# Linear attention and Sinkhorn-routed experts on one core: the attention front moved beside expert 0, and the expert loop turned outside in

## The chip, the cores and the metric

The kernel runs on one core of a Trainium2 chip. The metric is the device time of one execution in microseconds (us). The times of whole kernels are medians of executions; times within a kernel come from its one profiled execution. The engines are PE (TensorE, matmuls), PEld (its weight loads), DVE (VectorE), ACT (ScalarE), POOL (GpSimd) and SP (SyncE, here only an issuer of DMAs). SBUF is the working memory on the chip; the results of matmuls go to PSUM, here in banks of 128x512 fp32 values, and VectorE or ScalarE moves them from there to SBUF, which is called evicting. The granted clock is the share of TensorE's full clock that the profile shows as let through.

## The reference, cut to what matters

```python
q, k, v: (8 batches, 8 heads, 576, 64) fp32      # x below has N = 4608 rows of 512
phi(x) = where(x > 0, x, exp(x) - 1) + 1
kv  = einsum('bhsd,bhse->bhde', phi(k), v);  z = sum_s phi(k)
x   = einsum(phi(q), kv) / (einsum(phi(q), z) + 1e-6)     # heads side by side
P   = exp(x @ w_gate - max)                               # (4608, 8)
for _ in range(8):                                        # Sinkhorn
    P /= P.sum(1, keepdims=True) + 1e-9
    P /= P.sum(0, keepdims=True) + 1e-9
    P *= N / E
for e in range(8):                                        # every expert sees every row
    out += P[:, e:e+1] * (max(x @ w1[e], 0) @ w2[e])      # 512 -> 1024 -> 512
```

The experts are nearly all of the arithmetic: 8 experts, 9 groups of 512 rows, and 64 matmuls of 128x512 for each pair (32 that make `hq = x @ w1`, 32 that make `ye = relu(hq) @ w2`). `phi` of k is computed in both kernels as max(x + 1, exp(min(x, 0))): a min on VectorE, an exp on ScalarE, a max on VectorE. The changed kernel does q the same way.

## The kernel before

It has a front, the Sinkhorn iterations and an expert part, one after the other, and a scheduler orders the instructions. The front:

```python
for b in range(B):
    ...                                   # q: cast by DMA to DRAM as fp16, then a transposing DMA
    for rq in range(NR // 2):
        nc.sync.dma_start(out=k_q, ...)                       # fp32, runs of 256 bytes
        nc.gpsimd.dma_start(out=v_q[:, :, 0:D], ...)          # cast to fp16 on the way
        ...                                                   # phi of k
    for r in range(NR):
        ...                                                   # kv, num/den, division, transpose of x
```

The expert part takes three groups at a time and runs all experts over them, so that weights are loaded three times:

```python
for sg in range(NSG):                    # 3 supergroups
    for e in range(E):
        ...                              # load w1[e], w2[e]
        for gi in range(GSG):            # 3 groups of 512 rows
            ...                          # 32 hq and 32 ye matmuls, Relu on ScalarE
            for tt in range(4):          # ye has ONE set of four PSUM banks
                nc.vector.scalar_tensor_tensor(out=oacc[gi][:, tt, :], in0=ye_ps[:, tt, :],
                                               scalar=P_sb[:, gg, e:e + 1], in1=oacc[gi][:, tt, :], ...)
```

The softmax here doesn't subtract the row's maximum and nothing guards it: scores larger than these inputs give would overflow.

## Time and profile before

| what | before |
|---|---|
| time, median of 2 | 1229.8 us (1229.6 to 1229.99) |
| span of the profiled execution | 1228.2 us |
| front, to about | 204 us |
| period of one group of 64 matmuls | 13.97 us |
| PE busy | 89% of the span |
| granted clock, mean | 0.998 |
| read from HBM | 129 MB |

Three rows of the table of 40 slices on the page (each digit is a slice of 30.7 us, in tenths busy; GB/s is what the DMA engines moved):

```profile
PE   0162378999999999999999999999999999999997
...
DMA  9999991043044214433440343044434413440301
GB/s 163 161 150 161 157 106 11 1 69 63 6 69 69 44 25 69 69 91 81 69 69 5 65 69 57 13 69 73 100 68 69 69 18 52 69 69 3 67 31 73
```

Six slices in which DMA is at 9 and PE is between 0 and 7, then PE at 9 to the end. The front is about a sixth of the time, and it has DMA engines that are busy while they move only some 160 GB/s.

### The profile page before, as it was taken

What the parts mean: (1) busy time and instruction counts of PE and PEld (TensorE: products, weight loads), DVE (VectorE), ACT (ScalarE), POOL (GpSimd) and SP (SyncE); (2) the same over time, 40 slices, a digit from 0 to 9 for tenths busy, and PEclk for the clock granted to TensorE, in tenths of its full rate; (3) what the DMA queues carried; (4) which work ended last, traced back from release to release, by engine and by line L of the source; (5) the groups of instructions that cost most, each with busy time, mean ns of one, the idle gap of its engine ahead of it and who ended that gap; (6) DMA issues with size and microseconds to landing.
All of it is one profiled execution on the core that took longest, in us unless ns stands there. A gap on an engine that the chain in (4) does not pass through costs nothing.

```text
span 1228.2 us, 13108 instructions
## 1 busy us (share of the span) xinstructions
PE 1093.9 (89%) x5568; PEld 490.8 (40%) x5568; DVE 328.4 (27%) x634; ACT 415.1 (34%) x642; POOL 107.9 (9%) x119
## 2 busy tenths in 40 slices
PE   0162378999999999999999999999999999999997
PEld 0142255344444444444444444444444444444442
DVE  3264484831121111221112211122111221111211
ACT  2253332333333333333333333333333333333332
POOL 7461020000000000000000000000000000000000
PEclk9999999999999999999999999999999999999999
DMA  9999991043044214433440343044434413440301
GB/s 163 161 150 161 157 106 11 1 69 63 6 69 69 44 25 69 69 91 81 69 69 5 65 69 57 13 69 73 100 68 69 69 18 52 69 69 3 67 31 73
DMA packets 173274, 84.21 MB, mean 69 GB/s; under 512 B 131744, under 2 KB 156320, under 8 KB 173216
## 3 DMA queue, kind: packets, MB, share of 16 engines
q0 software_dynamic: 112656, 59.78, 38.5%
q1 hardware_dynamic: 60560, 23.60, 10.7%
q8 instruction: 43, 0.70, 0.2%
q14 instruction: 15, 0.12, 0.0%
HBM read 128.99 MB, written 14.16 MB: 117 GB/s over the span
## 4 chain that ended last, share of the span: by engine, by line
PE 81%; issue 6%; DMA 6%; POOL 4%; DVE 3%; ACT 0%; DVEq 0%; POOLq 0%; ACTq 0%
PE ye_ps L300 40%; PE hq L290 39%; DMA v<-in_v_dram 6%; POOL q L93 2%; POOL v L131 1%; DVE yst L309 0%; DVE gsum L246 0%; PE logits_ps L211 0%; POOL v L133 0%; DVE w_tmp L232 0%; DVE w_tmp L244 0%; DVE ut L235 0%; PE csum_ps L247 0%; PE num_ps L171 0%; DVE t L242 0%
## 5 line engine op out<-in xcount | busy, mean ns | idle before, releaser
L296 ACT ACTIVATE h_sb<-hq 128x512 f16<-128x512 f32 x576 | 343.7, 597 | 669.2 <-PE hq L290 669.2
L290 PE MATMUL hq<-xT,w_t 128*128 128x512 f16 x2208 | 524.6, 379 | 0.0
L300 PE MATMUL ye_ps<-w_t,h_sb 128*128 128x512 f16 x2208 | 523.1, 380 | 0.3 <-ACT h_sb L296 0.3
L315 DVE SCALAR_TENSOR_TENSOR oacc<-ye_ps,P_sb,oacc 128x512 f32<-128x512 f32 x252 | 171.8, 745 | 707.8 <-PE ye_ps L300 707.8
L300 PEld LDWEIGHTS <-h_sb 128*128 128x128 f16 x2304 | 205.0, 98 | 301.2 <-ACT h_sb L296 113.7
L290 PEld LDWEIGHTS <-w_t 128*128 128x128 f16 x2208 | 215.2, 97 | 264.3 <-issue 11.3
L158 PE MATMUL kv_ps<-v,kp_q 128*64 128x65 f16 (+1 forms) x320 | 24.8, 249 | 104.4 <-POOL v L133 103.9
L280 POOL DMA_DIRECT2D w_t<-in_moe_w_dram x23 | 17.3, 753 | 886.7 <-PE hq L290 886.7
L158 PEld LDWEIGHTS <-kp_q 128*64 128x64 f16 (+1 forms) x320 | 19.8, 143 | 108.9 <-issue 97.8
L93 POOL DMA_DIRECT2D q<-in_q_dram x32 | 45.1, 2792 | 0.2 <-issue 0.2
L201 ACT COPY xT<-xT_ps 128x576 f16<-128x576 f16 x32 | 20.2, 637 | 72.0 <-PE xT_ps L196 71.8
L196 PE MATMUL xT_ps<-ident,x_sb 128*128 128x128 f16 (+1 forms) x160 | 24.5, 292 | 16.6 <-DVE x_sb L187 7.8
L171 PE MATMUL num_ps<-kv_sb,qpTg 64*128 64x65 f16 (+1 forms) x320 | 35.2, 244 | 0.8 <-DVE kv_sb L165 0.8
L311 DVE TENSOR_SCALAR oacc<-ye_ps,P_sb 128x512 f32<-128x512 f32 x24 | 16.4, 744 | 67.5 <-PE ye_ps L300 67.5
L103 ACT ACTIVATE qT1g<-qTg 128x2304 f16<-128x2304 f16 x8 | 17.0, 2124 | 33.6 <-DMA qTg<-q 33.6
L187 DVE TENSOR_TENSOR x_sb<-num_ps,rden 128x320 f16<-128x320 f32 x64 | 27.8, 480 | 0.1
L171 PEld LDWEIGHTS <-qpTg 64*128 64x128 f16 (+1 forms) x320 | 24.0, 121 | 9.5 <-issue 0.9
L142 ACT ACTIVATE e_k<-m_k 128x1152 f16<-128x1152 f16 x16 | 18.4, 1164 | 23.3 <-DVE m_k L140 21.2
L131 POOL DMA_DIRECT2D v<-in_v_dram x16 | 25.1, 1571 | 3.5 <-POOL v L133 3.2
L300 PE MATMUL ye_ps<-w_pre,h_sb 128*128 128x512 f16 x96 | 25.0, 391 | 0.0
L196 PEld LDWEIGHTS <-x_sb 128*128 128x128 f16 (+1 forms) x160 | 14.3, 125 | 25.5 <-issue 12.2
L290 PE MATMUL hq<-xT,w_pre 128*128 128x512 f16 x96 | 24.4, 400 | 0.0
(50 smaller groups left out, 192.9 us busy)
## 6 DMA issues: line engine op xcount, KB each, us to landing
w_t<-in_moe_w_dram POOLq DMA_DIRECT2D x46, 1024.0 KB, 11.4
k<-in_k_dram SPq DMA_DIRECT2D x16, 576.0 KB, 11.2
out_dram<-oacc SPq DMA_DIRECT2D x9, 1024.0 KB, 5.1
q<-in_q_dram POOLq DMA_DIRECT2D x32, 144.0 KB, 13.7
v<-in_v_dram POOLq DMA_DIRECT2D x16, 288.0 KB, 12.9
w_pre<-in_moe_w_dram POOLq DMA_DIRECT2D x2, 1024.0 KB, 17.0
qTg<-q SPq DMA_TRANSPOSE x8, 13.4
wg_sb<-in_moe_w_gate_dram POOLq DMA_DIRECT2D x1, 8.0 KB, 4.7
```

Source lines behind the costliest of these rows:

```text
L93: nc.gpsimd.dma_start(out=q16[bq][ds(rq * S, S), :].rearrange("s (h d) -> s h d", h=2), in_=AP(tensor=q.tensor, offset=(bq * H + 2 * rq) * ...
L131: nc.gpsimd.dma_start(out=v_q[:, :, 0:D], in_=AP(tensor=v.tensor, offset=base, ap=[[D, P], [P * D, NJ2], [1, D]]))
L142: nc.scalar.activation(out=e_k, in_=m_k, func=AF.Exp)
L158: nc.tensor.matmul(kv_ps[64 * hh:64 * hh + 64, :], lhsT=kp_sb[r0:r1, j, :], rhs=v1_sb[r0:r1, j, :], start=(ci == 0), stop=(ci == len(ch) - 1),
L171: nc.tensor.matmul(num_ps[0:cols, hh, m * 65:(m + 1) * 65], lhsT=qpT_sb[64 * hh:64 * hh + 64, 128 * m:128 * m + cols], rhs=kv_sb[64 * hh:6 ...
L187: nc.vector.tensor_tensor(out=x_sb[:, :, 64 * hh:64 * hh + 64], in0=numv, in1=rden[:, hh, :, None].broadcast_to([P, NM, D]), op=ALU.mult,)
L196: nc.tensor.transpose(xT_ps[:, 128 * m:128 * m + rows], x_sb[0:rows, m, :], ident[0:rows, 0:rows],)
L201: nc.scalar.copy(out=xT_sb[r][:, S * b:S * b + S], in_=xT_ps)
L290: nc.tensor.matmul(hq_t[fi], lhsT=w1_t[:, rr, ts(f, P)], rhs=xT_sb[rr][:, ds(512 * g, 512)], start=(rr == 0), stop=(rr == NDT - 1),)
L296: nc.scalar.activation(out=h_sb[:, fi, :], in_=hq_t[fi], func=AF.Relu)
L300: nc.tensor.matmul(ye_ps[:, tt, :], lhsT=h_sb[:, fi, ds(P * tt, P)], rhs=w2_t[:, f, :], start=(Qq == 0 and fi == 0), stop=(Qq == 3 and fi ...
L315: nc.vector.scalar_tensor_tensor(out=oacc[gi][:, tt, :], in0=ye_ps[:, tt, :], scalar=P_sb[:, gg, e:e + 1], in1=oacc[gi][:, tt, :], op0=ALU ...
```

## The change

Its intent is to take the front off the path. q, k and v come as large fp32 loads on the SP queue (each partition reads whole rows), GpSimd casts v, PE transposes phi(q). Only batch 0 stands alone. The other seven batches are emitted as a generator, in stages, between the matmul steps of expert 0, which runs unscaled because P isn't known yet. Sinkhorn follows as the last stages of the same generator; then the accumulators of expert 0 are scaled, and experts 1 to 7 run over all nine groups each, adding into accumulators that stay in SBUF. Weights are read once. The order of every queue is manual. The diff, cut to its core:

```diff
+    ctx.enter_context(tc.manual_schedule())
+    ye = [yps.tile([P, 512], FP32, tag=f"ye{t}", name=f"ye{t}") for t in range(4)]
 ...
-                nc.sync.dma_start(out=k_q, in_=AP(tensor=k.tensor, offset=base,
-                                                  ap=[[D, P], [P * D, NJ2], [1, D]]))
-                nc.gpsimd.dma_start(out=v_q[:, :, 0:D], ...)
+        src = [[NJ * D, P], [2 * S * D, 2], [1, NJ * D]]
+        for nm, ten in (("k", k), ("v", v), ("q", q)):
+            nc.sync.dma_start(out=t.rearrange("p r j d -> p r (j d)"), in_=AP(tensor=ten.tensor, offset=off, ap=src))
 ...
+    def att(b, g):                      # one half batch (4 heads), in 8 stages
+        kp = phi(kin, "k")
+        for hh in range(2):
+            nc.gpsimd.tensor_copy(out=vv[64 * hh:64 * hh + 64, :, :, hh, 0:D], in_=vin[64 * hh:64 * hh + 64])
+        qp = phi(qin, "q")
+        yield
+        ...                             # kv | transposes of q | den, num, division | transposes of x
 ...
+    def side_work():
+        for b in range(1, B):
+            pair = [att(b, 0), att(b, 1)]
+            ...                         # the two half batches stage by stage, in turn
+            if b % 2 == 1:
+                yield from logits(b // 2)
+        yield from sinkhorn()
 ...
+    def run(units, hqpool, look, after):
+        for i in range(len(steps) + look):
+            if i < len(steps):
+                steps[i][0](steps[i][2])                  # 4 hq matmuls and a Relu
+            if i >= look:
+                after(i - look)
+                steps[i - look][1](steps[i - look][2])    # 4 ye matmuls (and the evictions, at f = 7)
+    RATE = 2.4                                            # stages of side work for each step
+    run([(0, g, w1c, w2c) for g in range(7)], hq2, 1, after0)
+    while not side_done[0]:
+        advance()
 ...
+    for e in range(1, E):
+        run([(e, g, w1c, w2c) for g in range(NG)], hq4, 3, lambda i: None)
```

## The prediction

> **What bounds the kernel now.** I read the page's table of 40 slices first, then the chain of waits, the table by stage, the groups, and last the timeline at three places. The table by stage (columns: stretch in us; busy us of PE, its weight load, VectorE, ScalarE, GpSimd with counts; granted clock; DMA share; GB/s):
>
> ```profile
> 100.00:150.00 50.00, 14.18 (x150) 10.30 (x150) 16.31 (x44) 12.77 (x12) 6.70 (x9) 1.00 1.52 164
> ...
> 215.00:240.00 25.00, 23.03 (x108) 9.78 (x107) 20.70 (x66) 7.16 (x12) 0.00 (x0) 1.00 0.00 0
> ...
> 400.00:600.00 200.00, 199.84 (x916) 85.06 (x915) 38.17 (x56) 68.13 (x115) 8.18 (x10) 1.00 0.36 67
> ```
>
> There are two kernels in one. Up to about 204 us the attention front runs and its stretches show no compute engine even half busy, while the DMA queues are full (the share column is above 1) at only 164 GB/s. From 204 us to 1219 us the PE is solid. The chain of waits says the same by line:
>
> ```profile
> PE ye_ps L300 40%; PE hq L290 39%; DMA v<-in_v_dram 6%; POOL q L93 2%; POOL v L131 1%; DVE yst L309 0%; DVE gsum L246 0%; PE logits_ps L211 0%; POOL v L133 0%; DVE w_tmp L232 0%; DVE w_tmp L244 0%; DVE ut L235 0%; PE csum_ps L247 0%; PE num_ps L171 0%; DVE t L242 0%
> ```
>
> The front waits for v (fp32 cast to fp16 by GpSimd-issued DMA in 256-byte runs), for q's prepass and its DMA transpose; everything afterwards is the two expert matmuls. In the steady part, the groups repeat every 13.97 us (in the chain in order of time the 14 hq matmuls that open a group start at 408.26, 422.23 and 436.20), so 13.97 / 64 matmuls = 0.2183 us per 128x512 matmul, and 8 experts x 9 groups x 13.97 = 1005.8 us. Front 204 + 1006 + 9 lost in the first groups (sinkhorn steps and a cold clock) + 9 of tail (1219 to 1228) makes the 1228 us span.
>
> One detail of the steady part decides my prediction. The timeline at a group boundary:
>
> ```profile
> 604.20 2.73 DVE L315 SCALAR_TENSOR_TENSOR oacc<-ye_ps,P_sb,oacc 128x512 f32<-128x512 f32 x4 [11.24 <-PE ye_ps L300]
> ...
> 604.00 3.23 PE L290 MATMUL hq<-xT,w_t 128*128 128x512 f16 x14
> 607.07 1.89 PE L300 MATMUL ye_ps<-w_t,h_sb 128*128 128x512 f16 x8
> ```
>
> The four evictions of ye need 604.20 to 606.93; ye has only one set of four banks. The scheduler put 14 hq matmuls (3.07 us) there, so the next ye matmul at 607.07 just doesn't wait.
>
> **What the Trainium skill says.** (1) "TensorE: Matmul & The Clock Gate", section Back-to-back issue gap: N/2.4 + 2.5 ns when warm, 216 ns at N=512. The trace agrees within 1.5% (218), so this term can't shrink. (2) Same page, Part 1: after about 3.4 us of idling the array runs at half rate until it has been busy about as long. The trace agrees: eight matmuls below take 3.58 us, about 0.43 each, at the end of the sparse front.
>
> ```profile
> 204.43 3.58 PE L290 MATMUL hq<-xT,w_pre 128*128 128x512 f16 x8
> ```
>
> (3) "DMA: Bandwidth & Descriptors", section SWDGE vs HWDGE vs iDMA: a cast during DMA exists only on the GpSimd path. That is why the old v and q loads sit there; plain fp32 loads can go to the SP queue. The trace has the SP store of 1 MB at 262 GB/s including its ends (1222 to 1226 us), against 164 in the front. (4) "Perfetto Trace Analysis", section Matmuls: independent matmul groups should rotate through PSUM banks so that evacuation overlaps the next group. Neither kernel does it for ye; before replaces it by the 14 hq matmuls, above.
>
> **The change, part by part.** Its order of instructions is manual. I read it from the built program.
>
> *Experts 1 to 7.* 63 groups x 13.97 = 880 us as before. But hq now runs only three tiles ahead, and between the last four ye matmuls of a group and the first four of the next stand only 4 hq matmuls; the ye matmuls wait on VectorE. Let 0 be the start of the last ye matmul on bank 0. Matmul start to eviction start is 0.41 us (the fourth bank's in the same timeline the last eight ye start at 602.27 and take 1.90: 602.27 + 1.90 less one matmul's recorded 0.38 is 603.79, eviction 604.20). Four evictions in 2.73 us with 0.745 for the last are 0.66 apart, so bank k is free at 0.41 + 0.66k + 0.745 + 0.04 = 1.20, 1.86, 2.52, 3.18. PE would come to bank k at 8 x 0.218 + 0.218k = 1.75, 1.96, 2.18, 2.40. Banks 2 and 3 are late; the loss is 3.18 - 2.40 = 0.78 us. At an expert's first group 16 hq matmuls stand there and nothing is lost. 7 x 8 boundaries x 0.78 = 44 us. **Sum 924 us.**
>
> *Front for batch 0, exposed.* Six loads of 590 KB at an estimated 330 GB/s (a weight load at 296 to 310 us writes 151 GB/s x 14 us = 2.1 MB of fp16, so reads 4.2 MB of fp32, in 0.94 x 14 = 13.2 us: 320) land one each 1.8 us from about 4.5 us. VectorE then runs four phi in a row. Rows:
>
> ```profile
> L144 DVE SCALAR_TENSOR_TENSOR kp_q<-k,e_k 128x1152 f16<-128x1152 f32 x16 | 21.6, 1351 | 5.0 <-ACT e_k L142 5.0
> ...
> L142 ACT ACTIVATE e_k<-m_k 128x1152 f16<-128x1152 f16 x16 | 18.4, 1164 | 23.3 <-DVE m_k L140 21.2 <-DVE rden L182 2.1
> ```
>
> min 0.76 (median of L140) + exp 1.16 + max 1.4 (two halves) + handovers 0.1 = 3.4 us each, strictly in series because VectorE's order is min, max, min, max: 13.7 us, to about 18.5. Transposes of q, num/den, transposes of x through two PSUM buffers and 637 ns ScalarE copies: some 12 us. **31 us.**
>
> *Batches 1 to 7 beside expert 0.* PE work per batch: 6.67 of the 8-matmul steps (16 generator stages at 2.4 per step) x 1.75 = 11.7 us, plus an estimated 6.6 us of attention (per half batch 9 kv matmuls of 260 columns at 260/512 x 0.218 = 0.11, and 39 small matmuls and transposes at about 0.06, a quarter of 0.218 for 128 columns: 3.3): 18.3 us. If PE bound, 7 x 18.3 = 128 us. But the queues are in order, and the four exps of the next batch stand behind this batch's x copies and two Relus, which wait for PE: exp starts 5.6 us after the last division (two steps, four x transposes, a Relu). The four phi then take 12.7 us; the Relus of later steps stand behind them, with only two hq buffers, so PE has one more step and the kv matmuls to do and stops for about 10 us. After kv's copies (0.4) come the q transposes, den, num and four steps: 12.3 us. 5.6 + 12.7 + 0.4 + 12.3 = **31 us a batch, 217 for seven**; four logits rounds add 6.
>
> *Sinkhorn.* Now 8 VectorE operations between PE sums; from the rows of before (458, 453, 378, 458, 670, small ones about 0.2, PE handover 0.49) 3.9 us an iteration against 4.76 before, 31 us in all. Before hid it behind the PE stream; here 9 stages stand within under 4 steps, so PE waits at each sum. With the 4 steps left over (7 us): **38 us.**
>
> *Groups 7 and 8 of expert 0:* **28 us.** The 36 scalings of accumulators (about 0.4 each, 14.4 us) lie beside expert 1's first 14 us. *Tail:* eviction 3.1 and small stores, **7 us** against 9.
>
> Sum: 31 + 217 + 6 + 38 + 28 + 924 + 7 = **1251 us**. So the hiding of the front (saves most of 204) is paid back by stalls in expert 0, an exposed sinkhorn and the ye boundary.
>
> **Rivals.** *A: PE bound beside expert 0.* If phi overlaps more than I think, a batch takes 18 to 22 us: 1160 to 1190 us. For it: summed busy times per batch are only about 15 us for VectorE and ScalarE. Against: the program order. *B: cold clock.* Stops of 10 us per batch should send the array to half rate for 3 to 4 us after each (0.43 us seen above); 2 us x 8 more, 1265 to 1270, more if it stays cold throughout. *C: DMA or GpSimd.* 3.5 MB per batch is 11 us at 330 GB/s, hidden in 31; but at batch 1 they share with 8 MB of weight reads, perhaps 5 to 10 us once. No row of before shows a GpSimd copy of 64x1152; at 8 us each (four a batch) it would become the bound and make 1290. *D: no boundary loss.* If the evictions free banks earlier, 44 us fall away: 1207.
>
> **Range and chances.** 1251 with B pulling up and A down. My serial chain is built by hand, so I leave wide room below: 1195 to 1285. More than 2% faster means under 1205, which needs both A in part and D, or A fully: 0.18. Within 2%, 1205 to 1254: 0.40. Slower: 0.42.
>
> **What would show it.** Right: ye groups in experts 1 to 7 repeat every 14.75 us with ye idle "<-DVE acc"; first hq near 31 us; expert 0's seven groups end near 285 us with PE under 65% busy and Relus waiting behind exps; expert 1 starts near 320. Wrong: a 13.97 us period (step of the boundary false), or expert 0 done before 250 us (serial chain false), or PE waiting on GpSimd or DMA per batch.

## The result, and the profile after

The changed kernel takes **1266.84 us** (1266.49 to 1267.18, 2 runs) against 1229.8, and its result is right. The ratio is 1.030 with a 95% interval of 1.027 to 1.033: slower by 3%.

The same rows of the table of slices, for the changed kernel (a slice is 31.6 us; PEclk is the granted clock in tenths):

```profile
PE   3766667676999999999999999999999999999997
...
PEclk9877888886999999999999999999999999999999
DMA  9733322100210012000400040004000400003333
GB/s 271 199 113 112 109 97 73 60 1 1 46 21 1 1 19 48 1 1 1 67 1 1 1 67 1 1 1 67 1 1 1 67 1 1 1 1 67 67 77 90
```

The DMA bound is gone: 271 GB/s in the first slice, and a share of 3 or less in the third to tenth. PE starts at once, but it is at 6 or 7 for nine slices, at a granted clock of 0.6 to 0.8. The table by stage (columns as in the prediction: stretch, its length, PE, PEld, DVE, ACT and POOL busy with counts, clock, DMA share, GB/s) has one batch, the Sinkhorn and the experts:

```profile
105.00:140.00 35.00, 22.99 (x187) 12.93 (x186) 16.93 (x28) 13.84 (x22) 5.61 (x4) 0.80 0.31 102
280.00:320.00 40.00, 25.80 (x93) 11.39 (x94) 24.58 (x69) 7.04 (x12) 0.00 (x0) 0.70 0.00 1
500.00:900.00 400.00, 387.54 (x1760) 171.87 (x1759) 76.32 (x112) 131.32 (x220) 4.91 (x6) 1.00 0.10 16
```

In the batch no engine is busy for more than 23 of 35 us: it is bound by a chain that runs through all of them. In the experts PE is busy for 387.5 of 400 us, where before had 199.84 of 200. The timeline at a group boundary there answers to the one that the prediction shows of before (start, duration, engine, line, operation, count, and in brackets the idle time before it and what ended it):

```profile
706.80 2.73 DVE L289 SCALAR_TENSOR_TENSOR acc<-ye,P_sb,acc 128x512 f32<-128x512 f32 x4 [11.91 <-PE ye L274]
...
706.38 1.03 PE L274 MATMUL ye<-w,h 128*128 128x512 f16 x4
707.24 1.03 PE L265 MATMUL hq<-xT,w 128*128 128x512 f16 x4
708.11 0.59 PE L274 MATMUL ye<-w,h 128*128 128x512 f16 x2
708.92 0.38 PE L274 MATMUL ye<-w,h 128*128 128x512 f16 x1 [0.22 <-DVE acc L289]
709.58 0.38 PE L274 MATMUL ye<-w,h 128*128 128x512 f16 x1 [0.28 <-DVE acc L289]
```

Between the last ye matmuls of a group and the first of the next stand 4 hq matmuls, where before had 14. Banks 2 and 3 aren't yet evicted when PE comes to them. Undisturbed, the four starts would be 0.216 us apart, so the fourth would start at 708.11 + 0.65 = 708.76; it starts at 709.58. That is 0.82 us lost, although the bracketed idle times add up to only 0.50: a matmul's recorded duration (0.38) is longer than its spacing, and hides part of a wait.

The chain of waits by engine (its shares of the span) answers to that of before, of which the prediction shows the shares by line (PE had 81% there, DMA 6, DVE 3):

```profile
PE 73%; DVE 18%; issue 4%; ACT 4%; DVEq 0%; DMA 0%; ACTq 0%
```

DMA has left the chain, and VectorE has come in: half of its 18% are evictions at the boundaries, the rest phi, division and Sinkhorn.

The stages, read from where their first and last instructions stand, against the terms predicted:

| stage of the changed kernel | predicted | measured |
|---|---|---|
| batch 0, to the first hq | 31 | 34.0 |
| batches 1 to 7 with the logits | 217 + 6 | 243.3 (34.0 to 277.3) |
| Sinkhorn and the steps beside it | 38 | 36.4 (to 313.7) |
| groups 7 and 8 of expert 0 | 28 | 27.8 (to 341.5) |
| experts 1 to 7 | 924 | 916 (to 1257.4) |
| tail | 7 | 8.0 |
| sum | 1251 | 1265.4 (the span) |

In the same terms, before spends 63 x 13.97 = 880 us on all but nine groups, 9 in the tail, and so 1228.2 - 889 = 339 us on the front, the Sinkhorn and nine groups. The changed kernel needs 341.5 for these. **So the whole gain of hiding the front is lost again inside the first 341 us**, and the experts then cost 36 us more (916 against 880). The experiments ask where each loss sits.

### The profile page after: what moved, and what is told of

Same layout as the page of the kernel before. It is cut to its first block, busy times and chain, and to the rows that moved or that the text cites. A ratio compares the mean times of both kernels' runs of the same rounds, so it can differ in the third digit from the quotient of the medians.

```text
span 1265.4 us, 13555 instructions
## 1 busy us (share of the span) xinstructions
PE 1116.9 (88%) x5536; PEld 516.0 (41%) x5536; DVE 346.6 (27%) x587; ACT 427.3 (34%) x695; POOL 62.2 (5%) x63
## 4 chain that ended last, share of the span: by engine, by line
PE 73%; DVE 18%; issue 4%; ACT 4%; DVEq 0%; DMA 0%; ACTq 0%
PE hq L265 35%; PE ye L274 34%; DVE acc L289 9%; DVE pk L106 2%; ACT mk L103 1%; ACT mq L103 1%; DVE pq L106 1%; DVE xn L159 1%; DVE mq L102 1%; PE xt_ps L169 1%; PE qt_ps L139 1%; DVE mk L102 1%; ACT h L268 1%; PE num_ps L157 1%; PE kv_ps L128 1%
## 5 line engine op out<-in xcount | busy, mean ns | idle before, releaser
L274 PE MATMUL ye<-w,h 128*128 128x512 f16 x2304 | 616.1, 384 | 30.2 <-DVE acc L289 27.9
L265 PE MATMUL hq<-xT,w 128*128 128x512 f16 x2304 | 597.0, 384 | 0.0
L268 ACT ACTIVATE h<-hq 128x512 f16<-128x512 f32 x576 | 343.9, 597 | 732.0 <-PE hq L265 731.6
L289 DVE SCALAR_TENSOR_TENSOR acc<-ye,P_sb,acc 128x512 f32<-128x512 f32 x252 | 171.7, 744 | 731.2 <-PE ye L274 731.2
L265 PEld LDWEIGHTS <-w 128*128 128x128 f16 x2304 | 227.6, 99 | 304.3 <-issue 44.8
L274 PEld LDWEIGHTS <-h 128*128 128x128 f16 x2304 | 225.4, 99 | 289.3 <-issue 38.0
L128 PE MATMUL kv_ps<-vv,pk 128*128 128x260 f16 x144 | 26.2, 345 | 67.1 <-DVE pk L106 67.1
L121 POOL CAST vv<-vin 64x1152 f16<-64x1152 f32 x32 | 41.7, 1302 | 176.8 <-DMA vin<-in_v_dram 169.8
L106 DVE SCALAR_TENSOR_TENSOR pk<-kin,mk 128x576 f16<-128x576 f32 x32 | 28.9, 944 | 59.7 <-ACT mk L103 59.7
L106 DVE SCALAR_TENSOR_TENSOR pq<-qin,mq 128x576 f16<-128x576 f32 x32 | 25.6, 841 | 20.3 <-ACT mq L103 20.3
L159 DVE TENSOR_TENSOR xn<-num_ps,rden 128x512 f16<-128x512 f32 (+1 forms) x48 | 26.7, 597 | 9.1 <-PE num_ps L157 7.9
L287 DVE COPY acc<-ye 128x512 f32<-128x512 f32 x18 | 11.7, 685 | 39.3 <-PE ye L274 24.1
```

The costliest lines, as they stand in the source:

```text
L106: nc.vector.scalar_tensor_tensor(out=o[:, :, r, :], in0=t[:, r], scalar=1.0, in1=m[:, r], op0=ALU.add, op1=ALU.max)
L121: nc.gpsimd.tensor_copy(out=vv[64 * hh:64 * hh + 64, :, :, hh, 0:D], in_=vin[64 * hh:64 * hh + 64])
L128: nc.tensor.matmul(kv_ps, lhsT=kp[:, j, :, :].rearrange("p r d -> p (r d)"), rhs=vv[:, :, j, :, :], start=(j == 0), stop=(j == NJ - 1))
L159: nc.vector.tensor_tensor(out=xn[:, i0:i1], in0=num_ps[:, 0:i1 - i0].rearrange("p i r h e -> p i (r h) e"), in1=rden[:, i0:i1, :, None].br ...
L265: nc.tensor.matmul(hp, lhsT=w1_t[:, c, ts(f, P)], rhs=xT[c][:, ds(512 * g, 512)], start=(c == 0), stop=(c == NDT - 1))
L268: nc.scalar.activation(out=h, in_=hp, func=AF.Relu)
```

## The experiments

Twelve kernels ran, each with three rounds against the kernel before, whose median lay between 1228.6 and 1230.2 us in all four sets. All are edits of the changed kernel. Three of them let GpSimd cast only a part of v and give a wrong result, as is said there; the others are correct. "Batch stretch" is the time from the first hq matmul to the end of the last logits exp, 243.3 us in the changed kernel.

### 1. Eight hq matmuls at a group boundary

Theory: the boundary loss comes from the order, because only 4 hq matmuls stand before ye is needed again. Rival: evictions come too late for another reason, and more hq matmuls there are needed elsewhere.

```diff
-            if i >= look:
-                after(i - look)
-                steps[i - look][1](steps[i - look][2])
+            while j < len(steps):
+                hold = 1 if (look == 3 and steps[j][2] == 0 and j > 0) else 0
+                if i < len(steps) and i - j < look + hold:
+                    break                    # a group's first ye waits for one hq step more
+                ...
+                after(j); steps[j][1](steps[j][2]); j += 1
```

> Only the order at a group's end in experts 1 to 7 is changed: 8 instead of 4 hq matmuls stand between the last ye matmuls of a group and the first of the next, with the same four ye banks. Theory of the boundary: PE reaches bank k at 12 x 0.216 + 0.216k = 2.59 to 3.24 us, after the banks are free (1.20 to 3.18), so the 0.83 us lost at each of 56 boundaries goes: 46 us, 1221 us in all, period 13.8 us, and no ye idle behind the evictions. Rival (the period is long for another reason, ScalarE's Relu or the matmul rate): less than 10 us gained. Nothing before 341 us should move.

Measured: **1219.39 us** (1219.13 to 1220.45), ratio to before 0.992 (0.990 to 0.993). The timeline at a boundary:

```profile
700.41 2.72 DVE L289 SCALAR_TENSOR_TENSOR acc<-ye,P_sb,acc 128x512 f32<-128x512 f32 x4 [11.09 <-PE ye L274]
...
699.99 1.03 PE L274 MATMUL ye<-w,h 128*128 128x512 f16 x4
700.85 1.89 PE L265 MATMUL hq<-xT,w 128*128 128x512 f16 x8
702.58 1.89 PE L274 MATMUL ye<-w,h 128*128 128x512 f16 x8
```

The eviction still takes 2.72 us, but eight ye matmuls follow eight hq matmuls without a wait. The group of all ye matmuls says it in sum, first for the changed kernel, then for this run (count, busy us, mean ns, then idle before them and what ended it):

```profile
L274 PE MATMUL ye<-w,h 128*128 128x512 f16 x2304 | 616.1, 384 | 30.2 <-DVE acc L289 27.9
```

```profile
L274 PE MATMUL ye<-w,h 128*128 128x512 f16 x2304 | 587.6, 384 | 2.3 <-ACT acc L285 1.2
```

The whole gain is 47.4 us. In the stage that the edit touches, from the first hq of expert 1 to the last ye, the time falls from 915.9 to 870.0 us, so 45.9 us are the boundary's (56 x 0.82 is 46); the rest lies before it, where nothing was changed. The recorded wait was 27.9 us: the theory holds, and the recorded idle time tells only some 60% of what such a wait costs. This edit alone already beats the kernel before.

### 2. The Sinkhorn iterations beside matmuls

Theory: the Sinkhorn stages are emitted almost without steps between them, so PE waits at each column sum. Given one stage per 2.4 steps (and groups 7 and 8 as cover), they cost nothing.

```diff
-        yield from sinkhorn()
+    RATE2 = 0.42                             # stages per step, once the batches are done
 ...
+        if side_done[0] and phase[0] == 0:
+            phase[0] = 1; side = sinkhorn(); side_done[0] = False; credit[0] = 1.0
+        credit[0] += RATE2 if phase[0] else RATE
 ...
-    while not side_done[0]:
-        advance()
+    run([(0, g, w1c, w2c) for g in range(7, NG)], hq2, 1, after0)
+    while not side_done[0]:
+        advance()
```

> Only the place of the sinkhorn is changed: its nine stages are emitted one per 2.4 steps, beside the rest of group 6 and groups 7 and 8 of expert 0, instead of 2.4 stages per step. Theory: its 32 us of VectorE chain then lie beside 20 steps x 1.73 = 35 us of PE work, and some 20 to 23 us of the 36 us between the last logits and group 7 are saved: 1245 us. Rival (the chain is on the path whatever stands beside it, because the scaling of expert 0 needs its result): under 5 us, and the wait turns up at the first eviction of expert 1.

Measured: **1245.18 us** (1244.75 to 1246.51), ratio 1.013 (1.011 to 1.014), 21.7 less than the changed kernel. The table by stage for the stretch shown above at 25.80 us of PE work and a clock of 0.70:

```profile
280.00:320.00 40.00, 37.74 (x182) 17.48 (x181) 25.74 (x71) 14.58 (x25) 0.72 (x1) 1.00 0.00 1
```

PE is at 37.74 of 40 us and the clock is back at 1.00, while VectorE does the same work. Confirmed.

### 3. Spare matmuls that keep PE warm (first form)

Theory: after its stop in each batch PE runs at half rate, some 2 us a batch. Rival: those slow matmuls lie beside the phi chain, which sets the pace anyway.

```diff
+        if b > 0 and g == 1:
+            for _ in range(48):              # overwritten by kv's start
+                nc.tensor.matmul(kv_ps..., lhsT=ident, rhs=xT[0][:, 0:4 * (D + 1)], start=True, stop=True)
         for j in range(NJ):
             nc.tensor.matmul(kv_ps, ...)
```

> 48 matmuls of identity on x (260 columns, about 5.2 us warm) are put before the kv matmuls of each second half batch, where PE waits about 6 us for k; their result is overwritten. Cold clock theory: in these waits the array drops to half rate and the next 10 to 12 long matmuls take 0.43 instead of 0.22 us, about 2.2 us a batch on the path; kept warm, 12 to 18 us are saved: about 1252 us, granted clock of 35 to 245 us from 0.82 to near 1. Rival (the in-order chain of phi alone sets the batch's length and the slow matmuls lie beside it): within 4 us of 1266.8, or a little slower.

Measured: **1264.09 us** (1263.44 to 1266.62), ratio 1.028 (1.027 to 1.030), 2.7 less. That is the rival's figure, and hardly more than noise: the batch stretch took between 241.5 and 243.3 us in the four profiles in which it is the same program (the changed kernel and experiments 1, 2 and 6), and 240.3 here. But the trace shows that the edit had missed part of its aim: after kv, PE stood for another 3.71 us (its wait for kvz), and the eight ye and hq matmuls that followed still took 1.91 us per four, as without the edit. So the question stayed open until experiment 9.

### 4. phi of the next batch in pieces

Theory: the batch is long because min, exp and max of four phi stand in one block in the VectorE and ScalarE queues, and the Relus behind them. Emitted in pieces between the stages of the batch before, the block is gone. Rival A of the prediction said the batches would be bound by PE then.

```diff
-        kp = phi(kin, "k")
-        ...                                  # cast of v, phi of q, in one stage
+    def phi_pieces(b, g):                    # m, exp | max, cast of v | m, exp | max, next loads
+        ...
+        order = {(0, 1): "0", (1, 0): "01", (1, 1): "1", (4, 1): "0", (5, 0): "01", (5, 1): "1"}
+            for rnd in range(7):
+                for x in range(2):
+                    next(pair[x])
+                    ...
+                    for c in order.get((rnd, x), ""):
+                        next(nxt[int(c)])    # a piece of batch b + 1
+                    yield
```

> Same operations, but the phi of batch b+1 is emitted in single pieces (min and exp, later the max) between the stages of batch b, instead of all four at the head of its own batch. In-order chain theory: 12.7 to 15 us of phi no longer stand alone between two batches; a batch falls from 34.7 us to 22 to 27 us (PE work 18.3, VectorE busy 15), and the result is 1190 to 1215 us. Rival (the engines' summed work or the clock, not the order, sets the batch): above 1245 us.

Measured: **1243.22 us** (1241.87 to 1247.0), ratio 1.011 (1.009 to 1.013): 23.6 less, and short of both expectations. The batch stretch ends at 244.8 instead of 277.3 us, 32.5 earlier. But a batch now has 14 stages instead of 16, so at the same rate fewer steps were done beside it: 176 hq matmuls in that stretch against 200 in the changed kernel. The missing 6 steps of 8 matmuls are 6 x 8 x 0.216 = 10.4 us that come after it, and 32.5 - 10.4 = 22.1 is about what was gained. The view of waits shows what took the place of the block (waiter, releaser, us in total, times, longest); first the changed kernel, then this run:

```profile
PE kv_ps L128 <- DVE pk L106: 67.1, 16, 11.7
```

```profile
PE kv_ps L144 <- DVE pk L109: 22.8, 4, 11.7
...
PE qt_ps L155 <- ACT qpT L116: 17.9, 10, 3.2
...
PE xt_ps L185 <- ACT xT L116: 10.9, 8, 2.9
```

The wait of kv for phi(k) falls from 67.1 to 22.8 us, and 28.8 us stand as waits for ScalarE's copies (2.6 in the changed kernel), before which the scattered exps now stand. The order was a cause, and the largest in the batches, but not one worth 50 us.

### 5. GpSimd casts only a ninth of v (wrong result)

In the changed kernel's trace some operations of phi were slow. Instruction by instruction, in one batch:

```profile
149.23 1.70 DVE L106 SCALAR_TENSOR_TENSOR pk<-kin,mk 128x576 f16<-128x576 f32 x1
...
150.85 1.73 DVE L102 TENSOR_SCALAR mq<-qin 128x1152 f16<-128x1152 f32 x1
...
149.08 1.24 POOL L121 CAST vv<-vin 64x1152 f16<-64x1152 f32 x1 [24.35 <-DMA vin<-in_v_dram]
...
150.38 1.58 POOL L121 CAST vv<-vin 64x1152 f16<-64x1152 f32 x1
```

The max takes 0.757 us in the median and the min 0.75; here they take 1.70 and 1.73. GpSimd's first cast ends at 150.32 and the max at 150.93; the second cast ends at 151.96 and the min at 152.58. So both VectorE operations end 0.61 to 0.62 us after the cast that ran when they were issued: they stood still for it. Over the whole kernel 13 operations of phi are slowed like this; each ends 0.60 to 0.62 us after a cast, and what they take beyond 0.755 us each is 12.7 us in sum. "SBUF — State Buffer", section Who interferes with whom, of the Trainium skill says so: a VectorE instruction with two SBUF inputs (the max) contends with a GpSimd instruction that reads SBUF, one in a two-port mode does as well, and the second to issue "fully blocks". That the min ran in such a mode no run shows; that it stood, the trace does. The prediction had looked at GpSimd only as an engine that might be too slow, and had not looked at this section.

```diff
-            nc.gpsimd.tensor_copy(out=vv[64 * hh:64 * hh + 64, :, :, hh, 0:D], in_=vin[64 * hh:64 * hh + 64])
+            nc.gpsimd.tensor_copy(out=vv[64 * hh:64 * hh + 64, :, 0:1, hh, 0:D], in_=vin[64 * hh:64 * hh + 64, :, 0:1])
```

> GpSimd casts only a ninth of v, so the result is wrong on purpose; every order, wait and matmul stays. Contention theory: in the changed kernel VectorE's max of a 128x576 pair takes 1.43 us alone and 2.37 us while GpSimd casts v, and the min 0.75 and 1.73; per half batch that is some 1.1 us on the phi chain, 15 to 17 us over eight batches: 1250 to 1254 us, and the mean of the kp max falls from 944 to about 760 ns. Rival (the slowed operations lie beside other waits, or slow for another reason): 1263 to 1268 us.

Measured: **1254.57 us** (1253.17 to 1255.78), ratio 1.020 (1.018 to 1.022), 12.3 less. The first hq comes at 31.0 instead of 34.0, the batch stretch is 234.6 instead of 243.3, together 11.7. The groups of the max, before and after the edit:

```profile
L106 DVE SCALAR_TENSOR_TENSOR pk<-kin,mk 128x576 f16<-128x576 f32 x32 | 28.9, 944 | 59.7 <-ACT mk L103 59.7
```

```profile
L106 DVE SCALAR_TENSOR_TENSOR pk<-kin,mk 128x576 f16<-128x576 f32 x32 | 23.3, 769 | 60.1 <-ACT mk L103 60.1
```

944 ns fall to 769. The interference theory holds, and the gain is about the 12.7 us counted above; the time was a little above its range.

### 6. Boundary and Sinkhorn together

> The boundary edit and the sinkhorn edit together. They act on different stages, so they should add up: 1266.8 - 47.4 - 21.7 = 1197.7 us, within 3. Rival (one shifts the wait into the other's stage): over 1203 us.

The edit is 1 and 2 together. Measured: **1199.15 us** (1198.23 to 1200.65), ratio 0.975 (0.973 to 0.977), 67.7 less than the changed kernel where the two parts alone gave 69.1. They add: they are different stages.

### 7. Boundary, Sinkhorn and phi in pieces

> Boundary, sinkhorn and phi-in-pieces edits together. In the phi run the batches ended 32.5 us earlier but the whole only 23.6 us, because the sinkhorn then stood longer alone. Theory: with the sinkhorn beside matmuls the whole 32 us come through, 1197.7 - 32 = 1166 us (1160 to 1170). Rival (gain of phi is 23.6 whatever the sinkhorn does): 1174 us. A third possibility, that phi and sinkhorn edits fill the same PE gaps: above 1180 us.

The edit is 1, 2 and 4, with `RATE = 2.2` (so more steps lie beside each batch: 192 hq matmuls in the batch stretch). Measured: **1180.27 us** (1178.12 to 1182.37), ratio 0.960 (0.958 to 0.962), correct. It gains 18.9 over the run with two edits, where phi in pieces alone gave 23.6. The time lies at the edge of the third possibility. My theory (32 us come through once the Sinkhorn is hidden) is wrong: the 10 us that experiment 4 had "lost" were never lost to the Sinkhorn, they were steps moved behind it, as the counts above show. I had read a shift of work as a loss. Why 18.9 and not 23.6 came through isn't shown; `RATE` was changed in the same run.

### 8. phi in pieces, with a ninth of v cast (wrong result)

> Phi in pieces, and GpSimd casting a ninth of v (result wrong on purpose). If what is left in the batches of the phi run is partly VectorE slowed by GpSimd on the path: 10 to 17 us below the phi run's 1243.2, so 1226 to 1233. If the path there is PE and ScalarE's queue: 1240 to 1244.

The edit is 4 and 5. Measured: **1233.17 us** (1231.61 to 1234.63), ratio 1.003 (1.001 to 1.004), 10.1 below experiment 4. Even with phi scattered, interference with GpSimd was on the path.

### 9. Spare matmuls, second form

The 48 spare matmuls of experiment 3, and 13 more after kv, into a PSUM tile that nobody reads:

```diff
+        if b > 0 and g == 1:
+            wp = hq2.tile([P, 512], FP32, tag="hq", name="hq")
+            for _ in range(13):
+                nc.tensor.matmul(wp, lhsT=ident, rhs=xT[0][:, 0:512], start=True, stop=True)
         yield
```

> The earlier warm run (48 spare matmuls ahead of the second kv of a batch) plus 13 spare matmuls after that kv, where PE still idled 3.71 us and ran the next ye and hq matmuls at 1.91 us per four instead of 1.03. Cold-clock theory: two such groups a batch are 1.76 us, seven batches 12 us, so some 12 below the warm run's 1264.1: 1250 to 1255 us. Rival (these matmuls lie beside ScalarE's copies and VectorE's kvz, which set the pace): 1260 to 1265 us.

Measured: **1258.85 us** (1257.26 to 1259.22), ratio 1.023 (1.021 to 1.026): 8.0 below the changed kernel, 5.2 below experiment 3. The timelines after kv, first of the changed kernel, then of this run:

```profile
155.86 0.71 PE L139 MATMUL qt_ps<-ident,pq 128*128 128x128 f16 x5 [2.74 <-DVE kvz L132]
156.37 1.91 PE L274 MATMUL ye<-w,h 128*128 128x512 f16 x4
158.07 1.91 PE L265 MATMUL hq<-xT,w 128*128 128x512 f16 x4
```

```profile
151.34 0.45 PE L147 MATMUL qt_ps<-ident,pq 128*128 128x128 f16 x5 [0.91 <-DVE kvz L136]
151.63 1.03 PE L282 MATMUL ye<-w,h 128*128 128x512 f16 x4
152.49 1.03 PE L273 MATMUL hq<-xT,w 128*128 128x512 f16 x4
```

The matmuls run at full rate, and the run lies between the two expectations. The cold clock costs 8 us in the batches, less than the 15 that I had counted from the slow matmuls (2.7 plus 12), I suppose because some of these matmuls lie beside ScalarE and VectorE work; no run separates them. The clock itself was cured: between 34 and 245 us it is 1.00, against 0.83 in the changed kernel. The 8 us are net of what the spare matmuls cost.

### 10. v cast by DMA instead of GpSimd

The three edits of experiment 7, and v loaded by a casting DMA that GpSimd issues, so that the result is right.

```diff
-            nc.gpsimd.tensor_copy(out=vv[64 * hh:64 * hh + 64, :, :, hh, 0:D], in_=vin[64 * hh:64 * hh + 64])
+            for r in range(2):
+                nc.gpsimd.dma_start(out=vv[64 * hh:64 * hh + 64, r, :, hh, 0:D],
+                                    in_=AP(tensor=v.tensor, ..., ap=[[NJ * D, PW], [D, NJ], [1, D]]))
```

> The three edits together, and v loaded by a casting DMA issued by GpSimd straight into its place, so no GpSimd cast runs and the result is right. If the cast's interference was what the cast run removed: some 10 to 12 below the three edits' 1180.3, so 1168 to 1171 us, and the mean of the kp max near 760 ns. Rival (issuing these DMAs holds GpSimd and slows VectorE as well, or v in short runs lands late behind the weights): 1178 us or more.

Measured: **1183.96 us** (1181.43 to 1186.94), ratio 0.963 (0.960 to 0.965), correct, and not faster than experiment 7. Both theories have a part. The mean of the kp max is 755 ns and the batch stretch 208.8 us instead of 218.6 in experiment 7, so the interference is gone and 9.8 us come. But the first hq comes at 45.8 instead of 34.0 us. From the view of waits:

```profile
PE kv_ps L148 <- DMA vv<-in_v_dram: 31.2, 2, 19.5
```

kv of batch 0 waits for v, which comes in 72 KB pieces in the same queue as 4 MB of weights.

### 11. Both costs of the batches away (wrong result)

> The cast edit (a ninth of v cast by GpSimd, result wrong on purpose) and both groups of spare matmuls together. If interference of GpSimd and the cold clock are two separate costs of the batches, they add: 1266.8 - 12.3 - 8.0 = 1246.5 us, within 3, and the stretch from the first hq to the last logits exp, 243 us in the changed kernel, becomes 226, near the 223 predicted. Rival (both lie in the same wait, so removing one hides the other): 1251 us or more.

The edit is 5 and 9. Measured: **1250.15 us** (1250.0 to 1250.43), ratio 1.016 (1.015 to 1.018), 16.7 less where the two alone gave 12.3 + 8.0 = 20.3. So they overlap by some 4 us, between theory and rival. The size is rough: the medians of before in these sets differ by up to 1.6 us. The batch stretch is 229.5 us (31.1 to 260.6). The first exps of batches 1 and 7 start at 35.20 and 228.51 us, so one batch takes 32.2 us; in the changed kernel they start at 37.05 and 244.95, 34.65 a batch.

### 12. v of batch 0 ahead of the weights

Experiment 10 with expert 0's weights issued after both halves of batch 0, and expert 1's weights after the seventh group.

> The DMA-cast run with v of the first batch issued ahead of expert 0's weights, and expert 1's weights after the seventh group. In the DMA-cast run the first hq came at 45.8 instead of 34.0 us because v's second half waited 19.5 us behind the weights, while the rest of the batches was 9.8 us shorter. Theory: first hq at 31 to 34, so 1180.3 - 9.8 - 0 to 3, 1167 to 1171 us, correct, the best of all. Rival (v in short runs is late by itself): 1177 us or more.

Measured: **1177.9 us** (1175.63 to 1178.03), ratio 0.957 (0.955 to 0.959), correct. The first hq comes at 40.0 us, not at 31 to 34: kv of batch 0 still waits for v, until 19.43 and 27.33 us. So the rival is nearer: v in short runs is late by itself in batch 0, where everything is loaded at once. A part of that is the issue itself: GpSimd issues the first piece of v at 8.24 us, behind its own memsets, and the eight pieces take it 6.39 us; no run separates the two. The batch stretch is 211.2 us. This is the fastest version that is right, 4.3% below the kernel before, but its interval touches that of experiment 7 (0.960, 0.958 to 0.962), so the two are about level.

## Why the prediction was right or wrong

The prediction said 1251 us and gave "slower by over 2%" the largest chance, 0.42; the kernel takes 1266.8, inside the range. The sum is 16 us low because the front took 23 us more than computed and the experts 8 us less, errors that partly cancel. By its own steps:

- **Experts 1 to 7, 924 us: right in mechanism and nearly in size.** The boundary waits on VectorE as described; I computed 0.78 us, the trace has 0.82 at the boundary shown, and removing the wait gave 45.9 us in its stage against the 44 computed. What I had wrong is the base of 880 us: without the boundary the 63 groups take 870.0 us. I read 13.97 us as 64 matmuls at 0.2183 each, but in before too most of them start 0.216 apart. Three times in a group a matmul comes some 0.05 us late and starts as ScalarE's Relu of the first of two hq tiles ends: twice a ye, whose weights are that tile, and once an hq, which writes into its buffer. Together that is 0.165 us a group, 10 us in 63. One of them, where ye starts 1.78 us after the first of eight hq instead of 1.73:

```profile
614.46 1.89 PE L290 MATMUL hq<-xT,w_t 128*128 128x512 f16 x8
615.59 0.60 ACT L296 ACTIVATE h_sb<-hq 128x512 f16<-128x512 f32 x1 [2.11 <-PE hq L290]
616.23 0.55 PEld L300 LDWEIGHTS <-h_sb 128*128 128x128 f16 x4 [0.38 <-ACT h_sb L296]
616.24 1.90 PE L300 MATMUL ye_ps<-w_t,h_sb 128*128 128x512 f16 x8
```

  The changed kernel makes hq three tiles ahead, and between 400 and 1200 us its trace has no spacing but 0.216 us and the two waits at a boundary. Rival D (no boundary loss) is dead.
- **Batch 0, 31 us: right without GpSimd.** It took 34.0. With the cast reduced it takes 31.0, so the missing 3 us are VectorE waiting for GpSimd.
- **Batches 1 to 7, 223 us with the logits: the mis-sized term.** It measured 243.3. The mechanism, four phi in a block that holds the exps, the Relus and PE, holds: the waits of kv for phi were 67.1 us, and scattering the block takes 19 to 24 us off the whole. (Before kv, PE stops for 5 to 8 us a batch, in two pieces, and not for about 10 at once.) What the step "the four phi then take 12.7 us" lacks is GpSimd's interference (8.7 us of the stretch, by experiment 5; from the first exp to the last max a batch takes 12.8 to 14.7 us, and 12.7 to 13.0 with the cast reduced), and what "q transposes, den, num and four steps: 12.3 us" lacks is the cold clock (8 us, by experiment 9; this was rival B, and its "2 us x 8" is twice too much). With both removed a batch takes 32.2 us. The prediction has 31 and 6/7 of a us for logits, 31.9, and the parts agree as well as the sum: in experiment 11 the four phi take 12.7 to 13.0 us (12.7 computed), and the first exp starts 5.5 to 6.5 us after the last division (5.6), save 8.4 and 8.9 in two batches that follow a round of logits. The hand-built chain was right for undisturbed engines. The stretch there is still 229.5 us against 223; 4.1 of these 6.5 us lie between the first hq and the first exp of batch 1. Rival B's total, 1265 to 1270, is met by luck: the cold clock is half of its 16 us, and GpSimd, which it didn't have, makes up the rest.
- **Sinkhorn, 38 us: right.** It took 36.4, and emitting it beside matmuls took 21.7 us off, as expected before that run.
- **Groups 7 and 8, and the tail: right** (27.8 for 28; 8.0 for 7).
- **The reading of the front of before was too even.** "No compute engine even half busy" holds for the stretch that the prediction shows, not for all of the front: from 61.4 to 92.1 us PE is busy for 18.8 and VectorE for 20.9 us of 30.7, from 153.5 to 184.2 us for 22.3 and 25.5. And the min on which "0.76" rests has that as its median, but a mean of 0.94 and a longest of 1.60 us: a sign that something can hold VectorE up (what it was there, no run shows), which the prediction left aside.
- **Rival A (PE bound beside expert 0)** was false for this program. It is not true of phi in pieces either: PE still waits there for ScalarE's copies. **Rival C** was false as put: the casts take 1.2 us in the median, not 8, and no queue of GpSimd is the bound. GpSimd did cost 12.3 us, through VectorE.

What stays open: the 4 us by which interference and cold clock overlap, and how far below 1178 us a better order of ScalarE's queue would go; no run moved the exps without moving stages too.

## What to carry to other kernels

Hiding a stage beside another only pays if the order of each in-order queue lets both go on: here a block of exps ahead of Relus made the front, the Sinkhorn and expert 0 together take 341 us, no less than the 339 us of the same work one after the other. When one set of accumulators is evicted at the end of a group, put as much independent PE work between groups as the whole eviction takes (eight matmuls for 2.7 us here, because the banks come free one by one), and don't trust the recorded idle time for the cost. Before moving a copy to GpSimd, look whether VectorE's operations beside it share its way into SBUF.

## What the Trainium skill lacked or had wrong

- "TensorE: Matmul & The Clock Gate", section Back-to-back issue gap, states a sustained 131 ns per matmul at N=512 for a stream of weight loads and matmuls, and calls 216 ns an overcount. Here such streams run at 216 ns per matmul (four in 0.86 to 0.87 us), in experiment 1 without a break from 400 to 1200 us; no run shows 131.
- The same page, Part 1, has the half rate after a stop, and the trace agrees (four matmuls of 128x512 take 1.70 us from start to start, 156.37 to 158.07, where they take 0.86 at full rate). Its cost under "Terms", throttled time times the share of the clock that is lost, is far too high here: a clock of 0.83 between 34 and 245 us is 72 us at half rate, an estimated 36 us by that rule. Counting slow matmuls gave 15 us; keeping the array warm gave 8.
- "SBUF — State Buffer", section Who interferes with whom, is right, and the prediction would have been better with it: each of 13 blocked operations ended 0.60 to 0.62 us after GpSimd's cast, though it takes 0.75 alone, so blocking is nearly complete, but some 0.14 us short of it.
- No page says what a single set of accumulators costs at the end of a group, or that PE's recorded idle time understates a wait: 27.9 us recorded were worth 45.9.
